# Holding four small loads of x back until Pool has cleared a tile, in a decode-attention kernel bound by its transfers

## The chip, the cores and the metric

The kernel runs on one core of a Trainium2 chip. The metric is the device time of one execution in microseconds (us). Times quoted are medians of several executions. A profile of one execution gives a *span*, from the first to the last instruction, which in most executions is about 1.3 us shorter than the measured time (362.7 us of span went with 363.97 us). All points in time below count from the start of the span.

## The reference

Two independent problems, A and B, of one decode step of attention each; their outputs are concatenated. All data are bf16.

```python
# for each of A and B:  x [2, 1, 576], k_cache and v_cache [2, 16, 16384, 128], wq [576, 4096], wo [4096, 576]
W = 4096                                     # only the last 4096 positions of the cache are used
q = (x @ wq)                                 # 32 heads of 128, two heads share one k/v head
scores = einsum(q, k[:, :, Sk - W:, :]) * 128 ** -0.5
p = softmax(scores)
o = einsum(p, v[:, :, Sk - W:, :])
out = o.reshape(2, 1, 4096) @ wo
```

x is 2.3 KB a problem. wq is 4.7 MB, wo 4.7 MB, and the used part of k and of v is 33.6 MB each. Both problems together read 153.1 MB, each byte once.

## The kernel before

The kernel lists its operations engine by engine, with dependences, and turns the dependences into semaphore waits; each engine executes its own list in order. What matters here is the start.

```python
def f_x(e):                                  # four small transfers: 2 problems x 2 copies, 2 rows of 1152 B each
    for P in range(NPROB):
        for h in range(2):
            last = e.dma_start(x8[4*P + 2*h : 4*P + 2*h + 2, :], probs[P][0][:, 0, :]).then_inc(x_sem, 16)
    return last
x_dma = dma_op("act", x_sem, 2 * NPROB, f_x, [], "x")            # on the ACT queue, waits for nothing

for P in range(NPROB):                                           # on the SP queue: wq of A, wq of B, 4.7 MB each
    ...
    wq_dma[P] = dma_op("sp", wq_sem[P], 1, f_wq, [], "wq%d" % P)

# Pool: ones, identities, then
p_zxU = pool(lambda e: e.memset(pTf[:, 0:XW].bitcast(FP32), 0.0), [], "zero_xU")
# ... sel, zero_zq
```

After that, x goes through a chain of small steps, and the chain releases further transfers:

```python
d_xs  = dve(... , [x_dma, d_hm], "xs8")          # DVE reads x
op_xT = tb_job(f_xT, ...)                        # PE transposes it
op_xev = act(f_xev, [op_xT, p_zxU], "xev")       # ACT puts it into the cleared xU
q_done[P] = pe(f_q, [wq_dma[P], op_xev], ...)    # PE: q = x @ wq, for A, then for B

# K and V come through a ring of 4 slots of 4.2 MB on the SP queue, in order: K0 K1 K2 K3 V0 K4 V1 ...
# wq of A and B (9.4 MB) lie in slots 0, 1 and 2 at the start, so:
first_deps = {0: [q_done[0]], 1: [q_done[0], q_done[1]], 2: [q_done[1]], 3: []}
# K0 goes to slot 3 at once; K1 (slot 0) waits for the q projection of A, K2 and K3 for that of B
```

For each K tile DVE transposes the two halves (`xt`), PE makes the scores (`st`), and so on; wo comes through the same SP queue in between.

## Time and profile before

| | before |
|---|---|
| time, median of the first three runs | 363.09 us |
| span of the profile | 362.7 us |
| SP queue's packets, share of the 16 DMA engines' span | 98.5% |
| PE, DVE busy | 65%, 58% |
| last x landed | 13.05 us |
| first K landed | 35.2 us |

These are lines of the page of the kernel before: part 1 (busy time) and the queue table of part 3 (packets, MB, share of the 16 engines' time). q1 is the SP queue, q10 the ACT queue.

```profile
PE 237.2 (65%) x1295; PEld 58.2 (16%) x935; DVE 211.9 (58%) x141; ACT 46.2 (13%) x80; POOL 22.1 (6%) x83
...
q1 hardware_dynamic: 6196, 153.10, 98.5%
...
q10 hardware_dynamic: 20, 0.01, 0.0%
```

Over the whole span no compute engine is near full; the 16 DMA engines are. The table of windows of the kernel before shows it by stage. Its columns are the stretch, its length, the busy time of PE, PEld (PE's weight loads), DVE, ACT and Pool, the clock granted to PE as a share of full speed, the share of the DMA engines' time, and GB/s. (A packet's whole time is counted in the window in which it starts, so a short window can show a share above 1.)

```profile
2.20:13.00 10.80, 0.00 (x0) 0.00 (x0) 0.00 (x0) 1.28 (x1) 2.01 (x5) 1.00 0.94 400
13.00:25.40 12.40, 10.45 (x45) 1.60 (x18) 2.68 (x7) 0.29 (x2) 1.14 (x5) 1.00 0.98 423
25.40:35.20 9.80, 8.09 (x38) 0.87 (x9) 0.00 (x0) 1.62 (x3) 0.00 (x0) 1.00 0.99 428
35.20:55.80 20.60, 15.76 (x62) 3.43 (x36) 17.59 (x5) 1.84 (x8) 1.59 (x6) 0.83 1.00 432
55.80:354.10 298.30, 196.80 (x1114) 49.61 (x833) 188.88 (x123) 40.80 (x66) 15.92 (x58) 0.85 1.00 430
354.10:362.70 8.60, 6.08 (x40) 2.65 (x39) 2.60 (x6) 0.40 (x1) 0.00 (x0) 0.60 0.53 210
```

From the second row to the fifth, the stream has no hole (0.98 to 1.00). At 354.1 us the last V has landed. So the time is the stream's start, the bytes at 430 GB/s, and a tail, in which PE finishes the last projection and the output is written.

The timeline of the kernel before shows the start. Rows of other engines are left out, and one row can merge neighbouring instructions of one line (start, length, engine, line, operation, count, and in brackets the idle time before it with what ended it; "q" behind an engine marks its queue's issue instructions):

```profile
0.80 0.81 ACTq L179 DMA_DIRECT2D tmp<-in_A_x_dram  x2
...
0.80 0.39 SPq L187 DMA_DIRECT2D ring<-in_A_wq_dram  x1
...
1.25 0.41 SPq L187 DMA_DIRECT2D ring<-in_B_wq_dram  x1
...
1.64 0.58 ACTq L179 DMA_DIRECT2D tmp<-in_B_x_dram  x2
...
1.84 0.34 POOL L201 MEMSET pT<- 128x288 f32 x1
...
13.08 1.34 DVE L217 TENSOR_TENSOR pR<-tmp,hmask 8x1152 bf16<-8x1152 bf16 x1 [11.52 <-DMA tmp<-in_B_x_dram]
...
15.65 0.59 PE L279 MATMUL ot<-ring,pT 128*32 128x512 bf16 x1 [0.47 <-ACT pT L265]
...
25.75 8.95 SPq L377 DMA_DIRECT2D ring<-in_A_k_cache_dram  x3
...
35.22 8.77 DVE L432 STREAM_TRANSPOSE xt<-ring 128x4096 f32<-128x4096 f32 x2 [19.46 <-DMA ring<-in_A_k_cache_dram]
...
45.63 8.77 DVE L432 STREAM_TRANSPOSE xt<-ring 128x4096 f32<-128x4096 f32 x2 [1.64 <-PE st L248]
```

x is issued beside wq (ACT from 0.80 us), but DVE can read it only at 13.08 us. PE then starts the q projection at 15.65 us, and its end lets the second K be issued at 25.75 us (that row merges the second, third and fourth K). The first K has been in the queue since 1.71 us and lands at 35.2 us, when DVE starts on it.

### The profile page before, as it was taken

Reading aid. Unit: us, or ns where it says so; the run is one execution under the profiler, and the core shown is the slowest. Engines: PE = TensorE matmul, PEld = TensorE weight load, DVE = VectorE, ACT = ScalarE, POOL = GpSimd, SP = SyncE. Lnnn points to the kernel's source line nnn. Section 1 sums busy time; section 2 is a strip of 40 time slices with the busy share of each in tenths; the row PEclk is TensorE's granted clock in tenths of the full one; section 3 lists DMA queues with packets and bytes.
Section 4 is the critical chain, followed back from the end, with each engine's and each line's share of the span. In section 5 each row is a group of like instructions: output and inputs, shape, how many; then the busy total and the mean of one; then the engine's idle time right before and its main releaser. Section 6 shows DMA issues by size and latency. Waiting matters only on the chain.

```text
span 362.7 us, 2629 instructions
## 1 busy us (share of the span) xinstructions
PE 237.2 (65%) x1295; PEld 58.2 (16%) x935; DVE 211.9 (58%) x141; ACT 46.2 (13%) x80; POOL 22.1 (6%) x83
## 2 busy tenths in 40 slices
PE   0397687767665868471696666562586677667666
PEld 0010111112111212020131211110112121112222
DVE  0201898495949392924919492942917658585522
ACT  1002100140041001300014001400005000500500
POOL 3100101100010001000010001000010001000000
PEclk9999698969898888986798989889789687889986
DMA  8999999999999999999999999999999999999995
GB/s 326 447 431 416 448 417 441 426 430 437 430 435 408 455 408 426 454 419 444 420 435 426 434 434 414 440 441 412 452 414 442 426 441 420 438 423 441 407 422 220
DMA packets 6228, 153.28 MB, mean 423 GB/s; under 512 B 700, under 2 KB 840, under 8 KB 1224
## 3 DMA queue, kind: packets, MB, share of 16 engines
q1 hardware_dynamic: 6196, 153.10, 98.5%
q8 instruction: 9, 0.15, 0.2%
q10 hardware_dynamic: 20, 0.01, 0.0%
q14 instruction: 3, 0.02, 0.0%
HBM read 153.10 MB, written 0.00 MB: 422 GB/s over the span
## 4 chain that ended last, share of the span: by engine, by line
DMA 48%; DVE 25%; PE 16%; issue 8%; ACT 1%; SPq 0%; POOL 0%; ACTq 0%
DMA ring<-in_B_k_cache_dram 25%; DVE xt L432 15%; DMA ring<-in_A_k_cache_dram 13%; DMA ring<-in_B_v_cache_dram 8%; PE st L248 5%; PE st L458 4%; DMA tmp<-in_B_x_dram 3%; PE pj L248 3%; DVE oR L564 2%; DVE mx L466 2%; DVE pT L505 2%; DVE tmp L557 2%; ACT pR L496 1%; PE ot L279 1%; PE pj L635 1%
## 5 line engine op out<-in xcount | busy, mean ns | idle before, releaser
L458 PE MATMUL st<-xt,zq 128*128 128x512 bf16 x256 | 122.6, 479 | 89.9 <-DVE xt L432 89.8
L432 DVE STREAM_TRANSPOSE xt<-ring 128x4096 f32<-128x4096 f32 x32 | 141.6, 4429 | 36.3 <-DMA ring<-in_A_k_cache_dram 20.8
L248 PE MATMUL st<-xt,zq 128*128 128x512 bf16 x256 | 121.2, 473 | 0.0
L496 ACT ACTIVATE pR<-st,bias 128x512 bf16<-128x512 f32 x32 | 40.0, 1415 | 217.7 <-DVE bias L489 217.7
L458 PEld LDWEIGHTS st<-xt,zq 128*128 128x128 bf16 x256 | 29.0, 113 | 212.7 <-DVE xt L432 106.7
L535 PE MATMUL ot<-ring,pT 128*32 128x512 bf16 x512 | 32.5, 395 | 6.9 <-DMA ring<-in_B_v_cache_dram 4.4
L489 DVE SCALAR_TENSOR_TENSOR bias<-vmask,tb,offm 128x4 f32<-128x4 f32 x8 | 1.8, 223 | 36.1 <-PE tb L486 36.1
L519 DVE TENSOR_REDUCE ssum<-tb 128x2 f32<-128x8 f32 x8 | 1.3, 162 | 36.0 <-PE tb L516 36.0
L505 DVE STREAM_TRANSPOSE pT<-pR 128x2048 bf16<-128x2048 bf16 x8 | 18.4, 2304 | 0.7 <-ACT pR L496 0.7
L424 POOL TENSOR_TENSOR zq<-qs,bmask 128x64 bf16<-128x64 bf16 x32 | 8.6, 292 | 165.7 <-PE st L248 143.8
L557 DVE SCALAR_TENSOR_TENSOR tmp<-ot,rsb,dmask 128x512 f32<-128x512 f32 x16 | 11.5, 719 | 8.5 <-PE ot L535 8.4
L535 PEld LDWEIGHTS ot<-ring,pT 128*32 128x32 bf16 x512 | 12.6, 99 | 22.0 <-DMA ring<-in_B_v_cache_dram 8.9
L564 DVE TENSOR_REDUCE oR<-tmp 128x128 f32<-128x512 f32 x15 | 15.6, 1042 | 0.5
L248 PE MATMUL pj<-ring,pT 128*32 128x512 bf16 x36 | 11.9, 417 | 0.0
L248 PE MATMUL pj<-wob,oM 128*2 128x288 bf16 x48 | 11.9, 286 | 0.0
L616 PE MATMUL pj<-wob,oM 128*2 128x288 bf16 x48 | 11.9, 286 | 0.0
L258 PE MATMUL tb<-ident_b,pR 8*128 8x8 bf16 x9 | 0.7, 198 | 14.5 <-DVE pR L217 14.5
L466 DVE TENSOR_REDUCE mx<-st 128x2 f32<-128x1024 f32 x8 | 9.7, 1214 | 0.1
L496 ACT ACTIVATION_READ_ACCUMULATOR pR<-st,bias 128x1 f32 x32 | 8.9, 278 | 0.0
L217 DVE TENSOR_TENSOR pR<-tmp,hmask 8x1152 bf16<-8x1152 bf16 x1 | 1.3, 1345 | 11.5 <-DMA tmp<-in_B_x_dram 11.5
L279 PE MATMUL ot<-ring,pT 128*32 128x512 bf16 x18 | 7.5, 419 | 0.5 <-ACT pT L265 0.5
L248 PE MATMUL st<-ring,pT 128*32 128x512 bf16 x18 | 7.3, 407 | 0.0
(69 smaller groups left out, 71.4 us busy)
## 6 DMA issues: line engine op xcount, KB each, us to landing
ring<-in_A_k_cache_dram SPq DMA_DIRECT2D x8, 4096.0 KB, 24.9
ring<-in_A_v_cache_dram SPq DMA_DIRECT2D x8, 4096.0 KB, 29.9
ring<-in_B_k_cache_dram SPq DMA_DIRECT2D x8, 4096.0 KB, 28.6
ring<-in_B_v_cache_dram SPq DMA_DIRECT2D x7, 4096.0 KB, 29.9
ring<-in_A_wq_dram SPq DMA_DIRECT2D x1, 4608.0 KB, 13.8
ring<-in_B_wq_dram SPq DMA_DIRECT2D x1, 4608.0 KB, 24.2
wob<-in_A_wo_dram SPq DMA_DIRECT2D x2, 2304.0 KB, 29.8
wob<-in_B_wo_dram SPq DMA_DIRECT2D x1, 2304.0 KB, 27.4
```

What stands on the lines that cost most here:

```text
L248: return e.add_instruction(mybir.InstMatmult(name=nc.get_next_instruction_name(), engine=mybir.EngineType.PE, ins=[e.lower_ap(mv_), e.lowe ...
L279: last = e.matmul(QB[c], wt, mv_, start=first, stop=True, skip_group_check=True)
L424: last = e.tensor_tensor(dst, src, msk, ALU.mult)
L432: Xop[(t, jh)] = dve(lambda e: e.transpose(xt[:, jh, :].bitcast(FP32).rearrange("p (kp x kt) -> p x kp kt", kp=2, kt=2), ring[:, r, jh * H ...
L458: last = e.matmul(ob, wt, mv_, start=first, stop=True, skip_group_check=True)
L466: ch[(G, "max")] = dve(lambda e: e.tensor_reduce(mx[:], st[:, :].rearrange("p (x t) -> p t x", t=2), AX.X, ALU.max), [Sop[(2 * G + 1, 1)]] ...
L496: last = e.activation(pR[:].rearrange("p (x k) -> p k x", k=4)[:, kv, :], st[:, :].rearrange("p (x t) -> p t x", t=2)[:, kv % 2, :], ACTF.Exp,
L505: pT_op[G] = dve(lambda e: e.transpose(pT[:, v, :].rearrange("p (w j q) -> p j w q", w=4, q=8), pR[:].rearrange("p (j w q) -> p j w q", w= ...
L535: last = e.matmul(OTB[32 * c:32 * c + 32, :], pT[:, v, base + 32 * c:base + 32 * c + 32], ring[:, r, jj * 128:(jj + 4) * 128], start=rd == ...
L557: evac_op[i] = dve(lambda e: e.scalar_tensor_tensor(tv, o, rsb[:, v, b:b + 1], dm, ALU.mult, ALU.mult), deps, "ev%d" % i)
L564: ch[(G, "red%d" % b)] = dve(lambda e: e.tensor_reduce(oR[:, b, :], tmp[:].rearrange("p (j d) -> p d j", j=4), AX.X, ALU.add), [evac_op[i] ...
L616: last = e.matmul(PJ[h], oM[:, j, :], mv_, start=start and j == 0, stop=True, skip_group_check=True)
```

## The change

The intent: the four x transfers wait on the ACT queue until Pool has cleared xU (the `MEMSET pT` line above, over at 2.18 us), so that the first wq transfer is prepared with no other load beside it. The texts call what prepares a transfer's packets the descriptor generator; that x and wq contend for it is a supposition.

```diff
-        x_dma = dma_op("act", x_sem, 2 * NPROB, f_x, [], "x")
 ...
         p_zxU = pool(lambda e: e.memset(pTf[:, 0:XW].bitcast(FP32), 0.0), [], "zero_xU")
+        x_dma = dma_op("act", x_sem, 2 * NPROB, f_x, [p_zxU], "x")
```

The order of instructions on every engine stays the same; the wait is all that is new.

## The prediction

> **What bounds the kernel now.** The stream of transfers from HBM. The page's queue table has the SP queue's packets at 98.5% of the 16 engines' span; in the table of windows the DMA share is 0.94 from 2.2 to 13 us, 0.98 to 25.4, and 1.00 (430 GB/s) from 55.8 to 354.1 us, while DVE is busy 58% and PE 65%. In the DMA records each engine takes one 36,864 B row of wq per packet, back to back at 1.364 us. So the time is: first packet at 1.8 us, a slow first round of wq packets (1.4 to 2.5 us each, starting between 1.8 and 2.8 us), an unbroken stream, and from 354.1 us a tail of 8.6 us (last V, projection, output).
>
> **What the change does.** No instruction or byte is added or removed, and no engine's arithmetic is reordered. The four x transfers (issued from 0.80 to 2.22 us in the timeline, 0.24 to 0.53 us each) wait for Pool's clearing of xU, which ends at 2.18 us. They will issue from about 2.25 to 3.6 us, behind both wq and the first K transfer.
>
> Gain: the first x packets (0.47 us on two engines, at 1.72 us) no longer precede wq; those engines begin wq at 2.2 and 2.4 to 2.8 us, the others from 1.81. Estimate from this: 0 to 0.5 us of stream start, 0.1 to 0.2 us at the end.
>
> Cost: x lands later. The Trainium skill, "DMA: Bandwidth & Descriptors", section "Queues, rings and completion order", says that an engine takes turns between queue rows packet by packet. The trace agrees: after the first, x's packets come once per wq packet (1.364 us), seven turns, so x lands at 13.05 us. Now the first x packet, too, meets a full wq queue. Estimate: two more turns, landing at about 15.8 us (14 to 17). PE's first q projection then starts near 18.4 instead of 15.65 us; its end, which releases the second K transfer, moves from about 25.5 to 28 us, the second q's from 33.5 to 36.
>
> **How much is on the critical path.** Nearly none of the cost. Two wq and the first K (13.6 MB) keep the engines busy until it lands at 35.2 us, so the second K, issued at 28, still meets 6 us of backlog; the third, at 36, meets the second. The first scores move from 39.7 to about 41.5 us; DVE's third K transpose, which waited for its transfer at 55.76 us, starts perhaps 0.5 us late. One to two transfers (10 to 20 us) are queued by then and DVE is idle 42% of the time, so this is made up.
>
> **Predicted time.** 362.9 us, range 361.9 to 364.2. Faster by over 2%: 1%; within 2%: 98%; slower by over 2%: 1%.
>
> **Right or wrong in the profile.** Right if: DVE's wait for x grows from 11.5 us to 13 to 15.5; PE's first q matmul starts 1.5 to 4 us later; the first wq lands up to 0.6 us earlier than 14.6; the first K lands within 0.6 us of 35.2; the DMA share stays 1.00 after 36 us; the tail is unchanged. Wrong in its main step if a hole opens in the DMA share between 30 and 60 us, if x lands after about 21 us (the second K would then be issued after the backlog drained), or if x lands earlier than before.
>
> **What would make it wrong.** A much longer wait of x behind the wq and K descriptors; or a startup gain over 1 us, if the slow first round of wq packets comes from x in the generator and not from the first reads themselves.

## The result, and the profile after

Ratios of times are computed as the mean time of one kernel's runs over that of the other's in the same rounds, so they are not quite the ratios of the medians quoted. Executions over 1.5% slower than the fastest of the same kernel are left out of the means.

| | before | after |
|---|---|---|
| median, 6 runs each | 363.12 us (363.01 to 364.5) | 363.26 us (363.16 to 363.68) |
| ratio to before | | 0.9999 (95%: 0.9984 to 1.0015) |
| span of the profile | 362.7 us | 362.4 us |
| last x landed | 13.05 us | 15.50 us |
| second K issued | 25.75 us | 27.96 us |
| first K landed | 35.20 us | 35.20 us |

The time is the same. The timeline of the changed kernel, in the lines that answer to those above (Pool's and SP's lines of the program have moved by one):

```profile
0.80 0.41 SPq L186 DMA_DIRECT2D ring<-in_A_wq_dram  x1
...
1.27 0.41 SPq L186 DMA_DIRECT2D ring<-in_B_wq_dram  x1
...
1.84 0.34 POOL L200 MEMSET pT<- 128x288 f32 x1
...
2.21 0.91 ACTq L179 DMA_DIRECT2D tmp<-in_A_x_dram  x2
3.16 0.59 ACTq L179 DMA_DIRECT2D tmp<-in_B_x_dram  x2
...
15.52 1.35 DVE L217 TENSOR_TENSOR pR<-tmp,hmask 8x1152 bf16<-8x1152 bf16 x1 [13.96 <-DMA tmp<-in_B_x_dram]
...
18.09 0.59 PE L279 MATMUL ot<-ring,pT 128*32 128x512 bf16 x1 [0.47 <-ACT pT L265]
...
27.96 8.95 SPq L377 DMA_DIRECT2D ring<-in_A_k_cache_dram  x3
...
35.23 8.77 DVE L432 STREAM_TRANSPOSE xt<-ring 128x4096 f32<-128x4096 f32 x2 [17.02 <-DMA ring<-in_A_k_cache_dram]
...
47.33 13.10 DVE L432 STREAM_TRANSPOSE xt<-ring 128x4096 f32<-128x4096 f32 x3 [3.33 <-PE st L248]
```

In this pair of traces everything that hangs on x is 1.7 to 2.5 us later: DVE's read of x by 2.44 us, the q projection by 2.44, the issue of the second K by 2.21, DVE's second K by 1.70. (Two later traces of the kernel before issued the second K at 27.20 and 26.07 us, so against those it is 0.8 and 1.9 us.) The two things that hang on the stream are not: the first K lands at the same time, and DVE goes from its second K to its third without a stop, where it had waited 1.36 us for a transfer before (it stands in one line of three transposes now), so most of the delay is gone by 60 us. The queue line of its page, and then its table of windows, show no hole:

```profile
q1 hardware_dynamic: 6196, 153.10, 98.5%
```

```profile
2.20:13.00 10.80, 0.00 (x0) 0.00 (x0) 0.00 (x0) 1.28 (x1) 2.03 (x5) 1.00 0.94 400
13.00:25.40 12.40, 8.00 (x35) 1.40 (x16) 2.68 (x7) 0.29 (x2) 1.15 (x5) 1.00 0.98 423
25.40:35.20 9.80, 9.80 (x47) 1.07 (x11) 0.00 (x0) 0.00 (x0) 0.00 (x0) 1.00 1.00 431
35.20:55.80 20.60, 15.19 (x59) 3.13 (x32) 17.24 (x4) 3.47 (x10) 1.59 (x6) 0.83 1.00 432
55.80:354.10 298.30, 200.13 (x1117) 50.20 (x837) 188.73 (x124) 40.90 (x66) 16.03 (x58) 0.84 1.00 430
```

One part of the page misleads here: the chain that ended last. These are its summaries, of before and of after:

```profile
DMA 48%; DVE 25%; PE 16%; issue 8%; ACT 1%; SPq 0%; POOL 0%; ACTq 0%
```

```profile
DVE 36%; DMA 28%; PE 23%; issue 8%; ACT 2%; POOL 1%; ACTq 0%; SPq 0%; DVEq 0%; POOLq 0%
```

The share of DMA is 20 points lower at the same time and with the same stream. The change need not have done it: two more traces of the kernel before have 41% and 54%, and a second one of the changed kernel has 48%. Probably, where a K lands at about the moment DVE gets free, which of the two "came last" turns on tenths of a microsecond. The shares of the chain can't be read as a bound here; the windows can.

### The profile page after: what moved, and what is told of

The parts are those of the page before. It is cut to its first block, busy times and chain, and to the rows that moved or that the text cites. A ratio compares the mean times of both kernels' runs of the same rounds, so it can differ in the third digit from the quotient of the medians.

```text
span 362.4 us, 2626 instructions
## 1 busy us (share of the span) xinstructions
PE 238.9 (66%) x1294; PEld 58.3 (16%) x935; DVE 211.4 (58%) x141; ACT 46.3 (13%) x80; POOL 22.3 (6%) x83
## 4 chain that ended last, share of the span: by engine, by line
DVE 36%; DMA 28%; PE 23%; issue 8%; ACT 2%; POOL 1%; ACTq 0%; SPq 0%; DVEq 0%; POOLq 0%
DVE xt L432 23%; DMA ring<-in_B_k_cache_dram 16%; DMA ring<-in_B_v_cache_dram 8%; PE st L248 8%; PE st L458 7%; PE pj L248 3%; DMA tmp<-in_B_x_dram 3%; DVE pT L505 3%; DVE oR L564 3%; DVE mx L466 2%; DVE tmp L557 2%; ACT pR L496 1%; PE ot L279 1%; PE pj L616 1%; PE pj L635 1%
## 5 line engine op out<-in xcount | busy, mean ns | idle before, releaser
L458 PE MATMUL st<-xt,zq 128*128 128x512 bf16 x256 | 123.8, 484 | 82.8 <-DVE xt L432 81.4
L248 PE MATMUL st<-xt,zq 128*128 128x512 bf16 x256 | 122.5, 478 | 0.0
L505 DVE STREAM_TRANSPOSE pT<-pR 128x2048 bf16<-128x2048 bf16 x8 | 18.4, 2304 | 0.7 <-ACT pR L496 0.7
L557 DVE SCALAR_TENSOR_TENSOR tmp<-ot,rsb,dmask 128x512 f32<-128x512 f32 x16 | 11.5, 718 | 7.7 <-PE ot L535 7.6
```

The source lines that it names most:

```text
L248: return e.add_instruction(mybir.InstMatmult(name=nc.get_next_instruction_name(), engine=mybir.EngineType.PE, ins=[e.lower_ap(mv_), e.lowe ...
L458: last = e.matmul(ob, wt, mv_, start=first, stop=True, skip_group_check=True)
L505: pT_op[G] = dve(lambda e: e.transpose(pT[:, v, :].rearrange("p (w j q) -> p j w q", w=4, q=8), pR[:].rearrange("p (j w q) -> p j w q", w= ...
L557: evac_op[i] = dve(lambda e: e.scalar_tensor_tensor(tv, o, rsb[:, v, b:b + 1], dm, ALU.mult, ALU.mult), deps, "ev%d" % i)
```

## The experiments

Theory A: the stream of transfers is full from its first packet to its end and sets the time; the change did not start it earlier; x's later landing costs nothing as long as the second K is issued before wq and the first K have drained. Rival B: the stream did start earlier, and the later x took as much back. Rival C: the early stage is bound by the path from x through q to the second K, and the stream has slack. Rival D: x can be arbitrarily late, DVE and PE make it up.

All timed runs were compared with the kernel before on the same chip: "after" with 6 runs of it, after_again, no_x, wq_late and x_late_1 with 11 (median 363.44 us), the other four with another 11 (median 363.40 us). The traces give the rest:

| run | time, median | ratio, 95% interval | first wq packets, mean start of 16 | x landed | second K issued | first K landed | last V landed |
|---|---|---|---|---|---|---|---|
| before, three traces | | 1 | 2.12, 2.02, 2.08 | 13.05, 13.82, 14.07 | 25.75, 27.20, 26.07 | 35.20, 35.11, 35.11 | 354.07, 354.32, 354.37 |
| after | 363.26 | 0.9999 (0.9984 to 1.0015) | 2.14 | 15.50 | 27.96 | 35.20 | 354.11 |
| after_again | 363.35 | 0.9998 (0.9986 to 1.0010) | 2.04 | 15.52 | 27.77 | 35.03 | 354.29 |
| no_x | 363.47 | 1.0002 (0.9987 to 1.0016) | 2.05 | none | 24.76 | 35.12 | 354.01 |
| x_double | 363.32 | 0.9994 (0.9979 to 1.0009) | 2.10 | 13.87 | 26.51 | 35.08 | 354.23 |
| wq_late | 365.47 | 1.0053 (1.0041 to 1.0066) | 3.45 | 3.23 | 26.29 | 36.41 | 355.58 |
| x_late_1 | 363.23 | 0.9997 (0.9985 to 1.0010) | 2.07 | 18.17 | 30.35 | 35.08 | 354.22 |
| x_late_4 | 366.17 | 1.0069 (1.0054 to 1.0084) | 2.10 | 21.10 | 34.02 | 35.22 | 355.94 |
| x_late_6 | 369.42 | 1.0158 (1.0134 to 1.0182) | 1.98 | 25.11 | 37.98 | 35.00 | 359.85 |
| x_late_12 | 374.14 | 1.0290 (1.0270 to 1.0310) | 2.09 | 29.99 | 43.43 | 35.23 | 365.32 |

(A "mean start" is the mean over the 16 engines of the moment when each begins its first packet of wq, from the DMA records of the trace. "Landed" is the last semaphore update of a transfer in the trace.)

### after_again: the changed kernel once more

No edit.

> The changed kernel once more, unaltered, beside the kernel before on one chip, for a narrower interval. Theory A (the transfer stream binds, the later x is absorbed by the transfers queued behind wq, and the first wq packets did not start earlier): ratio to before 0.9990 to 1.0010, that is within 0.4 us. Rival B (an earlier start of the stream gains and the later x costs, and the two cancel by chance): also within 0.4 us; this run alone does not tell them apart. In the trace: x lands near 15.5 us, first K at 35.2 us.

Measured: ratio 0.9998 (0.9986 to 1.0010), x at 15.52 us. The two sets of runs agree; a gain or loss beyond about half a microsecond is excluded.

### no_x: x without transfers (wrong result)

```diff
-        x_dma = dma_op("act", x_sem, 2 * NPROB, f_x, [], "x")
+        x_dma = S.add("dve", lambda e: e.memset(x8[:, :], 0.1), [], "x_const")
```

> Wrong result on purpose: the four x transfers are taken away and x8 is filled with 0.1 on DVE, so x costs neither descriptors nor waiting. This bounds what any placing of x can gain. Theory A: the first wq packets still start at a mean of about 2.1 us and the first wq lands at 14.6 us (within 0.2), q starts when wq has landed, and the time is within 0.4 us of before. Rival B (x at the descriptor generator delays the stream): the mean first wq packet or the first wq's landing comes 0.4 to 1 us earlier, the first K lands before 34.8 us, and the time falls by as much, to 362.1 to 362.7.

Measured: ratio 1.0002 (0.9987 to 1.0016). (The comparison with the reference called even this output correct. It is not the function asked for; that comparison is too coarse to tell it.) DVE's and PE's lines in the timeline of this run:

```profile
1.59 1.34 DVE L217 TENSOR_TENSOR pR<-tmp,hmask 8x1152 bf16<-8x1152 bf16 x1
...
14.54 0.61 PE L279 MATMUL ot<-ring,pT 128*32 128x512 bf16 x1 [10.63 <-DMA ring<-in_A_wq_dram]
...
35.14 8.77 DVE L432 STREAM_TRANSPOSE xt<-ring 128x4096 f32<-128x4096 f32 x2 [30.87 <-DMA ring<-in_A_k_cache_dram]
```

x is ready 11.5 us earlier than before, the q projection now waits for wq alone, and the second K is issued 1.0 to 2.4 us earlier than in the three traces of before. The first K still lands at 35.1 us, and the time does not move. With no x transfer at all, the first wq packets start at 2.05 us on average, as they do with x ahead of them, and take 2.1 us each, as slow as before. This is the most that any placing of x could bring: nothing that these runs resolve (a gain over 0.5 us is excluded; the predicted 0.1 to 0.2 us could hide in the interval, but no landing shows it). Rival B's gain of 0.4 to 1 us is not there, and Rival C falls.

### x_double: four more small transfers behind x

Right behind the x transfers, ACT issues the same four reads again, into a part of the wo tile that is free until later. Left out below: the last of DVE's early masks and the first wo transfer wait for these reads.

```diff
+        x2_dma = dma_op("act", x2_sem, 2 * NPROB, f_x2, [], "x2")      # f_x2: as f_x, into wob[0:8, 0, :]
```

> The kernel before with the suspected cost doubled: right behind the four x transfers, ACT issues four more of the same reads into a part of the wo tile that is free until later. Theory A: the mean start of the 16 first wq packets stays at 2.0 to 2.2 us, the first K lands at 35.0 to 35.4 us, time within 0.4 us of before. Rival B (small transfers on the ACT queue take the descriptor generator from the first wq transfer): the first wq and the first K land 0.3 to 1 us later and the time rises by as much.

Measured: mean start 2.10 us, first wq landed at 14.47 us (before: 14.59, 14.50, 14.50), first K at 35.08 us, ratio 0.9994 (0.9979 to 1.0009). Doubling the suspected cost shows neither in the landings nor in the time. The Trainium skill, page "DMA: Bandwidth & Descriptors", section "Issuing engines are not separate DMA queues", says that initiating DMAs on several engines at once only saves the issuing sequencer's time, since they share the same 16 DMA engines. The runs agree as far as they go: SP issues wq at 0.80 us in every one of them but wq_late, whether or not ACT issues x beside it, and x's packets go between those of wq on the same engines (shown below). x on the SP queue was not tried.

### before_look1, before_look2: two more traces of the kernel before

> The kernel before, unaltered, for another trace of its start. Six traces without x ahead of wq so far have the mean start of the 16 first wq packets at 1.98 to 2.14 us and the first K complete at 35.00 to 35.23 us; the two with x ahead have 2.10 and 2.12 us, and 35.08 and 35.20 us. Theory A (x ahead costs the start nothing that can be seen): here again 1.98 to 2.14 us and 35.0 to 35.25 us. Rival B (x ahead of wq delays it): above 2.14 us, or the first K after 35.25 us.

> The same as the run before it, once more. Theory A: 1.98 to 2.14 us and 35.0 to 35.25 us. Rival B: above 2.14 us, or the first K after 35.25 us.

Measured: mean starts 2.02 and 2.08 us, first K at 35.11 us in both. So with x ahead of wq, four traces have 2.02 to 2.12 us; with x behind or absent, seven have 1.98 to 2.14. The change did not start the stream earlier by anything that shows beside this scatter. The mean of 16 alone would be a blunt test, since 0.3 us on two engines moves it by only 0.04 us (an estimate); the landing of the first wq, which waits for the last engine, says the same: 14.59, 14.50 and 14.50 us before, 14.59 and 14.40 after, 14.49 without x. x's landing in the kernel before turned out to vary, 13.05 to 14.07 us, so the change makes x 1.4 to 2.5 us later, not a fixed 2.45.

### wq_late: the reverse order

x is issued at once, and the two wq wait for the clearing of xU.

```diff
-            wq_dma[P] = dma_op("sp", wq_sem[P], 1, f_wq, [], "wq%d" % P)
 ...
         p_zxU = pool(... "zero_xU")
+            wq_dma[P] = dma_op("sp", wq_sem[P], 1, f_wq, [p_zxU], "wq%d" % P)
```

> The reverse order: x is issued at once as in the kernel before, and both wq and all behind them wait for the clearing of xU. The first wq is issued at 2.2 instead of 0.80 us. Theory A (the stream runs without a hole from its first packet to the end, so its start is on the critical path one for one): time up by 1.4 us over before (1.0 to 1.8), first K lands at 36.6 us, although x lands much earlier than 13 us (3 to 10 us). Rival C (the early stage is bound by the path x, q, second K, and the stream has slack): time unchanged or lower, since x lands earlier.

Measured: 365.47 us, ratio 1.0053, which is 1.9 us over before (1.5 to 2.4). Lines of its timeline:

```profile
2.20 0.40 SPq L200 DMA_DIRECT2D ring<-in_A_wq_dram  x1
...
3.25 1.35 DVE L217 TENSOR_TENSOR pR<-tmp,hmask 8x1152 bf16<-8x1152 bf16 x1 [1.70 <-DMA tmp<-in_B_x_dram]
...
36.44 4.45 DVE L432 STREAM_TRANSPOSE xt<-ring 128x4096 f32<-128x4096 f32 x1 [30.49 <-DMA ring<-in_A_k_cache_dram]
```

x lands at 3.23 us, ten microseconds earlier than before, and the kernel is slower. The first wq packets start 1.38 us later (3.45 against the mean of 2.12, 2.02 and 2.08), the first K lands 1.27 us later, and the last V 1.33 us later (355.58 against the mean 354.25). A later start of the stream arrives at the end of it undiminished. The measured time rose by 1.9, outside my 1.0 to 1.8, and more than this accounts for; the interval reaches down to 1.5.

The end of the traces shows where up to 1 us can come from, whatever the change. The last part of wo lands at 361.19 us in wq_late and at 359.70, 359.95 and 359.98 before, so 1.3 us later too. After it the program runs on for 3.1 us in wq_late, and for 3.0, 2.6 and 2.1 us in the traces of before. Over all 12 traces this tail is 2.1 us where the clock granted to PE in the last 5 us was 0.99 or 1.00 (five traces), and 2.6 to 3.1 us where it was 0.64 to 0.75 (the other seven). That this is the excess in the timed runs is not shown, since only one execution of wq_late was traced.

A late start delays PE and DVE as much as the stream, so wq_late alone does not tell which of them sets the time. x_late_1, next, does.

### x_late_1, x_late_4, x_late_6, x_late_12: x later and later

As the changed kernel, but x waits for Pool to clear zq n + 1 times (1.06 us each) as well, n being the number in the name.

```diff
-        p_zq = pool(lambda e: e.memset(zq[:]..., 0.0), [], "zero_zq")
+        for k in range(n + 1):
+            p_z = pool(lambda e: e.memset(zq[:]..., 0.0), [p_z], "zero_zq%d" % k)
+        p_zq = p_z
+        x_dma = dma_op("act", x_sem, 2 * NPROB, f_x, [p_zq], "x")
```

> As the changed kernel, but x waits for two clearings of zq on Pool as well, so it is issued near 5.2 us instead of 2.2 and should land near 18.5 us instead of 15.5. Theory A: the second K is then issued near 31 us, 2 us or more before the engines run dry (first engine at 34.0 us), so the time stays within 0.4 us of before. Rival B: each microsecond of later x costs one, so 3 us over the changed kernel, about 366.2 us.

> As the changed kernel, but x waits for five clearings of zq on Pool, so it is issued near 8.5 us and should land near 21.3 us. From the runs so far: the second K is issued 12.2 to 12.5 us after x lands, so near 33.6 us; first packets follow an issue by 1.0 us; the engines run dry between 34.0 and 34.8 us. Theory A: this is the knee: a hole of 0 to 1 us, time 0.2 to 1.0 us over before. Rival B (each microsecond of later x costs one): 8 us over before. Rival D (DVE and PE have enough slack that x can be this late and later at no cost): within 0.4 us here and in the next two runs.

> x waits for seven clearings of zq, is issued near 10.6 us and lands near 23.3 us; the second K is issued near 35.6 us. Theory A: the engines are dry for some 2 to 3 us after the first K, and the stream never makes this up: 2 to 3.5 us over before (365.3 to 366.9 us). Rival B: 10 us over. Rival D: within 0.4 us.

> x waits for thirteen clearings of zq, is issued near 17 us and lands near 29.3 us; the second K is issued near 41.6 us. Theory A: a hole of some 8 to 9.5 us after the first K, all of it in the time: 8 to 10 us over before (371 to 373.5 us), and x_late_12 minus x_late_6 equals the difference of their x landings to within 0.7 us. Rival B: 16 us over. Rival D: within 1 us.

Measured over before, from the ratios: x_late_1 -0.1 us (-0.5 to +0.4), x_late_4 +2.5 (2.0 to 3.1), x_late_6 +5.7 (4.9 to 6.6), x_late_12 +10.5 (9.8 to 11.3; 4 runs). DVE's second K, and the first half of its third, in x_late_1:

```profile
49.59 13.10 DVE L435 STREAM_TRANSPOSE xt<-ring 128x4096 f32<-128x4096 f32 x3 [5.71 <-PE st L251]
```

DVE starts its second K 4.0 us later than in the first trace of before, its third at 58.29 us instead of 55.76, and is still 2.5 us behind at 81 us; the last V lands at 354.22 us all the same, and the time is that of before. So the compute engines have slack and the stream has none. Windows of x_late_1 (first fence), x_late_4 (second), x_late_6 (third) and x_late_12 (fourth), with the DMA share and GB/s last:

```profile
33.00:35.00 2.00, 2.00 (x11) 0.19 (x2) 0.00 (x0) 0.00 (x0) 0.00 (x0) 1.00 1.00 426
35.00:37.00 2.00, 2.00 (x11) 0.29 (x3) 1.90 (x1) 0.00 (x0) 0.00 (x0) 1.00 1.18 508
```

```profile
33.00:35.00 2.00, 2.00 (x11) 0.19 (x2) 0.00 (x0) 0.00 (x0) 0.00 (x0) 1.00 0.50 213
35.00:37.00 2.00, 2.00 (x11) 0.20 (x2) 1.75 (x1) 0.00 (x0) 0.00 (x0) 1.00 0.88 262
```

```profile
33.00:36.00 3.00, 3.00 (x15) 0.39 (x4) 0.98 (x1) 0.00 (x0) 0.00 (x0) 1.00 0.26 109
36.00:39.00 3.00, 3.00 (x16) 0.29 (x3) 3.00 (x1) 0.00 (x0) 0.00 (x0) 1.00 0.00 0
39.00:42.00 3.00, 3.00 (x16) 0.39 (x4) 3.00 (x2) 0.00 (x0) 0.00 (x0) 1.00 0.96 350
```

```profile
33.00:36.00 3.00, 3.00 (x9) 0.30 (x2) 0.75 (x1) 0.00 (x0) 0.33 (x2) 1.00 0.23 98
36.00:39.00 3.00, 3.00 (x10) 0.25 (x2) 3.00 (x1) 0.00 (x0) 0.00 (x0) 1.00 0.00 0
39.00:42.00 3.00, 3.00 (x16) 0.29 (x3) 3.00 (x2) 0.00 (x0) 0.00 (x0) 1.00 0.00 0
42.00:45.00 3.00, 3.00 (x16) 0.39 (x4) 2.02 (x1) 0.00 (x0) 0.00 (x0) 1.00 0.48 131
```

The shape is a flat piece and a slope. At 18.17 us the second K is issued at 30.35 us, the engines are still on the first K, and it is free. At 21.10 us there is a hole. (An estimate from these runs: the engines run dry from 34.0 us, the first packet comes 1.3 us after the issue, and the issue 12.0 to 13.4 us after x lands, so the hole begins when x lands after some 19 to 21 us.) The second half of Rival B (every microsecond of x costs one) fails at x_late_1, Rival D at x_late_4.

My sizes for x_late_4, x_late_6 and (by less) x_late_12 were too small, and the traces say why in part. In x_late_4 the second K was issued at 34.02 us, near my 33.6, but its first packet came 1.34 us later where I had counted 1.0, so the engines were idle for 1.17 us on average; and the 16 packets after the hole took 1.77 us on average where the usual packet of 32,768 B takes 1.216. The sum, 1.17 + 0.55 = 1.7 us, is what the last V shows (355.94 against 354.25, +1.7). The time rose by 2.5: the tail after the last wo is 3.0 us in this trace, where it is 2.1 to 3.0 in those of before; whether that is the rest stays open. In x_late_6, x also landed 1.8 us later than I had estimated, at 25.11; its hole is 5.45 us and its last V comes 5.6 us late. In x_late_12 the hole is 10.71 us and the last V comes 11.1 us late. x_late_12 minus x_late_6 is 4.7 us in the medians against a difference of 4.9 us in the landings of x, as expected, but partly by luck: the issues of the second K differ by 5.45 us and the last V by 5.5, and the tail of the traced execution was 3.0 us in x_late_6 and 2.1 in x_late_12.

The restart also bears on a question that the prediction left open: why the first round of wq packets is slow (2.1 us on average before, where later ones take 1.364). In x_late_12 the stream restarts at 44.75 us, when x has been in place for 15 us and no other load is being issued, and of the 16 engines' first packets after the hole 14 again take 1.73 to 2.05 us instead of 1.216. The other two began some 0.7 us later and took 1.21. In x_late_6 eight took 1.92 to 2.07 us, and the eight that began 0.7 us later took 1.21 to 1.38. In each case all 16 ended within 0.25 us of each other. With no_x, where the slow first round comes without any x, this shows that small transfers are not needed for it. What makes it slow no run here shows.

## Why the prediction was right

- *The bound.* Right. wq_late delays the stream's start by 1.38 us and everything to the last V by 1.33; x_late_6 and x_late_12 put a hole in the stream, of 5.45 and 10.71 us, and take 5.7 and 10.5 us longer; x_late_1 delays PE and DVE but not the stream, and takes no longer. One detail was wrong: the last V does not end the stream, wo does, 5.6 us later.
- *x lands later, at about 15.8 us (14 to 17).* Right: 15.50 and 15.52. The Trainium skill ("DMA: Bandwidth & Descriptors", section "Queues, rings and completion order") has an engine take turns between queue rows packet by packet. The records agree: in the changed kernel, on the two engines that carry x, each of the eight packets per engine (four of data, four of semaphore updates) goes after a wq packet of 1.364 us, except two that met between one wq packet and the next at the change from the first wq to the second. When x runs alone, in wq_late, all four have landed 1.0 us after the last of them finished issuing (2.21 to 3.23 us).
- *q projection near 18.4 us, second K near 28 us, first scores near 41.5 us.* Measured: 18.09, 27.96, 41.23 us.
- *The cost is off the critical path, and x would have to land after about 21 us to hurt.* Right in kind, perhaps a little late in place: free at 18.17 us, but 2.5 us (1.7 at the last V) at 21.10 us. The knee is between the two.
- *The gain, 0 to 0.5 us of stream start and 0.1 to 0.2 us at the end.* This one term did not show: the first wq landed at 14.59 us before and after, and with x absent, behind or ahead, the mean start of the first wq packets is the same within the scatter of 1.98 to 2.14 us. The two engines that carry x did start their wq later in the trace of before, but the engines' starts are spread over about a microsecond anyway (1.81 to 2.84 us before, 1.82 to 2.92 after), and some other engine is last.
- *Predicted 362.9 us; measured 363.26.* Inside the range; the missing gain is smaller than what the runs resolve. The range held "no change" too, so the number alone would be a weak test; the landings of x, q and K are the better one.

## What to carry to other kernels

Before reordering small loads at the start, find out which later transfer hangs on them and how long the queue ahead of it lasts: here, as long as that transfer was issued before the queue drained, the load's latency was free, and past that point each microsecond cost about one. In a kernel like this, whose stream never stops, an order of issue pays only if it makes the first byte of the stream earlier; measure that from the first packets of several traces, since one trace scatters by as much as the gain hoped for. Taking the suspected cost out altogether, even with a wrong result, bounds the whole family of such changes in one run.

## What the Trainium skill lacked or had wrong

- No page that I consulted gives a cost for restarting a stream that has been idle. Here, in the first round after a hole, all 16 packets in x_late_4 took 1.64 to 1.99 us, 8 of 16 in x_late_6 1.92 to 2.07 and 14 of 16 in x_late_12 1.73 to 2.05, against 1.216 us in the steady stream (the others began 0.7 us later and took 1.21 to 1.38). On average over the 16 that is 0.45 to 0.6 us for each hole beside the hole itself. (Belongs to "DMA: Bandwidth & Descriptors".)
- "DMA: Bandwidth & Descriptors", section "Queues, rings and completion order", gives the turn-taking but not what it costs a small load: here each of four small transfers put a data packet and a semaphore packet on two engines, and each such packet that met the wq queue waited out a wq packet of 1.364 us, so data issued at 0.80 to 2.22 us landed at 13.05 to 14.07 us behind wq, and at 3.23 us ahead of it.
- The same page's section "SWDGE vs HWDGE vs iDMA" describes a packet, for the software path, as preferably at most 4096 B; here, on the hardware path, the records show one row of 36,864 B (1.364 us) as one packet and one turn.
- The same page's first table gives about 0.6 us to the first byte for this kind of issue. It does not say from when that counts. Here wq's first packet started 1.01 to 1.04 us after the start of its issue instruction and 0.61 to 0.64 us after its end, which agrees if it counts from the end; for the second K after the holes it was 1.31 to 1.34 us after the start and 0.78 to 0.81 us after the end.
